# A Linformer attention and squared-ReLU network: attention visits spread over a batch's 56 steps, k and v projected a batch ahead, inverse rows in four buffers

## The chip, the cores and the metric

The kernel runs on one core of a Trainium2 chip. The metric is the device time of one execution in microseconds (us). Three runs of the kernel before gave 481.41, 481.42 and 482.23 us, a median of 481.42 us. One further execution was profiled; all lines of the profile are of that one. The engines are TensorE (PE, with its weight loads shown as PEld), VectorE (DVE), ScalarE (ACT), GpSimd (POOL) and SyncE (SP). The last two do little here but issue transfers; a "q" behind an engine's name marks its queue.

## What is computed

```python
batch, n_heads, seq, head_dim = (8, 8, 1024, 64)
k_proj = 64
...
k_proj = np.einsum('ks,bhsd->bhkd', E, k)
v_proj = np.einsum('ks,bhsd->bhkd', F, v)
scale = 1.0 / np.sqrt(q.shape[-1])
scores = scale * np.matmul(q, k_proj.transpose(0, 1, 3, 2))
scores = scores - np.max(scores, axis=-1, keepdims=True)
attn = np.exp(scores)
attn = attn / (np.sum(attn, axis=-1, keepdims=True) + 1e-09)
return np.matmul(attn, v_proj).astype(np.float32)
...
x = np.ascontiguousarray(attn_out.transpose(0, 2, 1, 3)).reshape(B * S, H * D)
...
h = np.maximum(x @ w_in, 0.0)
return (h * h @ w_out).astype(np.float32)
```

An attention over 64 projected keys for each of 8 batches and 8 heads gives an x of 8192 rows by 512. Two products follow, to 2048 columns with a squared ReLU and back to 512. Matmuls run in bf16.

## The kernel before

**Tiles.** A batch has 1024 rows of x, kept transposed as `xT`, and is worked off in two chunks of 512. The first product makes `h` from `xT` and `w_in`, the second makes the output from `h` and `w_out`. For batch 0 and the first product of chunk (1, 0) these are plain sums over four or sixteen blocks (`first_plain`, `second_cold`). All later ones are done in Strassen's way: seven products of half-size blocks instead of eight, with sums of blocks (`x_sum`, `s`, `w_in_sum`, `w_out_sum`) made on VectorE.

**A first product.** `Group` has one method for each of the seven products, p1 to p7. Each writes 4 matmuls of 128x256 into a PSUM bank. p1's result is copied by ACT (L677) to a second bank, `chain`, into which p6, p7 and p4 add. p5's and p6's results are copied to SBUF by ACT as tiles `u` (`keep`, L544), and p3 and p7 finish with a VectorE instruction, `relu_sum` (L666), that adds such a `u` to a bank. p2 and p4 finish with a ReLU on ACT (L662). In every second group VectorE also squares `h` and makes the sums `s`, all recorded through one helper line, L150. A group is seven steps. p4 of a group comes as the third step of the next one, so it stands three steps behind its own p7, whose `relu_sum` reads the bank that p4 adds into.

**A second product.** `second_spread` cuts the seven products into quanta of 4 matmuls (L572), one or two to a step, in banks `ps_second`. `put` takes a finished quarter to a tile `o_sb` (ACT's copy L562, or VectorE's addition in L150) and stores it from SyncE's queue (L566). Within 28 steps, puts stand at about 8 and 28 on ACT and 20 and 24 on VectorE. The last chunk runs `second_seven`; its last put is made in two halves, one by ACT (L562) and one by VectorE (L560).

**Steps.** From the second chunk of batch 1 on, `both` issues at each step one quantum of a first and one of a second product. A batch is 56 steps, and step t+1 of the loop over b begins at t = 56(b-1). What else TensorE does is put at a step with `at` or `on`, and is issued after that step's matmuls. TensorE's order is thus written out by hand (`tc.manual_schedule`). The other engines' orders are made by the framework's scheduler, and on each engine instructions run in that order.

**Attention, as visits.** `project` (L258, L259) multiplies k and v by E and F; VectorE and ACT copy the result to `kp` and `vp` (L246, L247, L251, L252). `transpose_k_dma` (L295) and `transpose_q_dma` (L321) are transposing DMAs from SyncE's queue. `scores` (L329) is followed by ACT's exponential (L343). `sums` (L363) adds up the exponentials of two pairs of heads, and ACT makes the inverse rows twice (L367 to L369); VectorE fills in the missing rows by copies (L373). `sums_spread` (L382) makes them once (L386, L387) into a tile `inv`, and eight DMAs (L393) from SyncE's queue copy them to two tiles `rs`. `values` (L405) is followed by two VectorE multiplications with `rs` into `xT` (L409). `sum_x` makes four x_sums. In the stage of 56-step batches all visits share one pair of PSUM banks, `ps_att`, so each waits for the one before to be read.

**Buffers.** `part` holds the tiles `u` in five buffers, `outp` the tiles `o_sb` in three, tag `rs` of `soft` has three. There is one buffer each for the loaded K, V and Q of a batch and for `qT`, and two for `kp`, `kT`, `vp` and `xT`. K, V and Q are loaded from GpSimd's queue (L89).

**Order of visits before, for the loop's b.** Scores 3 of batch b+1 at t+1, q transpose of b+2 at t+2, sums_spread 2 at t+3, values 0 to 3 at t+7, 10, 20 and 23, both sum_x at t+24; then for batch b+2: project at t+30, k transpose at t+32, scores 0 to 2 at t+44, 47 and 53, sums_spread 0 at t+50. K and V of b+3 are loaded from t+34.

Of the kernel before, what the change touches and what calls it, by code (L numbers as in the profile page):

```python
# [9 lines left out]
P = 128  # L10
# [9 lines left out]
def kernel(  # L20
# [19 lines left out]
    NI = 8  # L40
# [23 lines left out]
    part_pool = ctx.enter_context(tc.tile_pool(name="part", bufs=5))  # L64
    out_pool = ctx.enter_context(tc.tile_pool(name="outp", bufs=3))
# [31 lines left out]
    e_f32 = soft_pool.tile([KP, S], F32, tag="rs", name="e_f32")  # L97
    nc.sync.dma_start(e_f32[:], E[:])

    k_f32 = soft_pool.tile([P, 2, NI, D], F32, tag="rs", name="k_f32")  # L100
# [121 lines left out]
    class Attention:  # L222
# [123 lines left out]
        def inverse(self, ps):  # L346
            rs = soft_pool.tile([P, 2, TCH], F32, tag="rs", name="rs")
            nc.scalar.activation(rs[:], ps[:], AF.Ln)
            nc.scalar.activation(rs[:], rs[:], AF.Exp, scale=-1.0)
            return rs  # L350
# [6 lines left out]
        def sums(self, pr):  # L357
# [8 lines left out]
            rs = [soft_pool.tile([P, 2, TCH], F32, tag="rs", name="rs") for _ in range(2)]  # L366
# [9 lines left out]
        def sums_spread(self, pr):  # L376
# [8 lines left out]
            inv = soft_pool.tile([P, 2, TCH], F32, tag="rs", name="inv")  # L385
            nc.scalar.activation(inv[:], ps[:], AF.Ln)  # L386
            nc.scalar.activation(inv[:], inv[:], AF.Exp, scale=-1.0)  # L387
            for j in range(2):
                rs = soft_pool.tile([P, 2, TCH], F32, tag="rs", name="rs")
                for a in range(2):  # L390
                    have = 32 * (2 * a + j)
                    for to in (64 * a, 64 * a + 32):
                        nc.sync.dma_start(rs[to:to + 32], inv[have:have + 32])  # L393
# [44 lines left out]
    class Chunk:  # L438
# [103 lines left out]
        def keep(self, ps):  # L542
            u = part_pool.tile([P, DM], F32, name="u")
# [99 lines left out]
    class Group:  # L643
# [35 lines left out]
        def p5(self):  # L679
            self.other = bank(n=turn["bank"] + 2)  # L680
            self.product(5, self.other, True)
            self.kept5 = self.chunk.keep(self.other[:])

        def p6(self):
            self.product(6, self.chain)
            self.u2 = self.chunk.keep(self.chain[:])
# [21 lines left out]
    with tc.manual_schedule(engines={PE}):  # L708
# [81 lines left out]
        at(45, nxt.sums, 0)  # L790
        at(47, nxt.scores, 2)
        at(49, nxt.scores, 3)
        at(50, nxt.values, 0)
        at(52, nxt.values, 1)
        at(53, nxt.sums, 2)
# [11 lines left out]
        at(1, nxt.transpose_k)  # L807
        at(3, nxt.scores, 0)
        at(5, nxt.scores, 1)
        at(7, nxt.sums_spread, 0)  # L810
        at(9, nxt.scores, 2)
        at(11, nxt.scores, 3)
        turn["pairs"] = 1
        run_all(chunk[1, 0].first_plain())
# [45 lines left out]
        def on(step, b, name, *args):  # L860
            at(step, lambda: getattr(atts[b], name)(*args))

        for b in range(1, B - 1):
            t = 56 * (b - 1)
            if b > 1:
                on(t + 1, b + 1, "scores", 3)
            on(t + 3, b + 1, "sums_spread", 2)
            on(t + 7, b + 1, "values", 0)
# [52 lines left out]
```

## Time and profile before

| | |
|---|---|
| median of three runs | 481.42 us |
| the profiled execution | 482.35 us |
| its span, first to last instruction | 480.5 us |
| one batch of 56 steps (186.64 to 242.50 us) | 55.86 us |
| in it busy: PE, PEld, DVE, ACT | 55.57, 44.80, 43.43, 35.78 us |
| granted TensorE clock | 1.00 throughout |
| DMA, mean over the span | 139 GB/s |

The page lists for each engine its busy time, share of the span and instructions. Groups of instructions stand by source line, with the tile written, an arrow, and the tiles read; behind the bar come busy time, the mean of one in ns and the idle time before them with what ended it. The timeline has start, length, engine, line and tiles, and in brackets the idle time before the instruction and who ended it; matmuls that follow one another are merged ("x4"). The chain of waits goes back from the end, at each step to what released the work, and is shown in order of time. Matmul ends are modelled, so that distances between starts say more than idle times. All VectorE sums and squares carry the line L150 of their helper and are told apart by their tiles.

### The profile page before, as it was taken

Reading aid. Unit: us, or ns where it says so; the run is one execution under the profiler, and the core shown is the slowest. Engines: PE = TensorE matmul, PEld = TensorE weight load, DVE = VectorE, ACT = ScalarE, POOL = GpSimd, SP = SyncE. Lnnn points to the kernel's source line nnn. Section 1 sums busy time; section 2 is a strip of 40 time slices with the busy share of each in tenths; the row PEclk is TensorE's granted clock in tenths of the full one; section 3 lists DMA queues with packets and bytes.
Section 4 is the critical chain, followed back from the end, with each engine's and each line's share of the span. In section 5 each row is a group of like instructions: output and inputs, shape, how many; then the busy total and the mean of one; then the engine's idle time right before and its main releaser. Section 6 shows DMA issues by size and latency. Waiting matters only on the chain.

```text
span 480.5 us, 10027 instructions
## 1 busy us (share of the span) xinstructions
PE 470.4 (98%) x4106; PEld 351.5 (73%) x4106; DVE 350.7 (73%) x613; ACT 287.2 (60%) x466; POOL 32.4 (7%) x45
## 2 busy tenths in 40 slices
PE   8999999999999999999999999999999999999996
PEld 3444445537878788787878778887887778888885
DVE  2456897956996679767897579966797678967671
ACT  2464467397547774678546785477745775565641
POOL 7310010200010000100010000100000000000000
PEclk9999999999999999999999999999999999999999
DMA  9999998999949496767939499495811054101012
GB/s 184 204 205 206 221 164 150 168 230 189 197 86 168 122 201 163 119 134 186 196 103 182 93 220 175 96 160 139 203 56 55 23 132 111 67 23 67 24 65 89
DMA packets 80046, 66.98 MB, mean 139 GB/s; under 512 B 30720, under 2 KB 76032, under 8 KB 80000
## 3 DMA queue, kind: packets, MB, share of 16 engines
q0 software_dynamic: 30640, 29.23, 39.4%
q1 hardware_dynamic: 49216, 36.97, 29.2%
q8 instruction: 32, 0.52, 0.4%
q10 hardware_dynamic: 144, 0.13, 0.1%
q14 instruction: 14, 0.11, 0.1%
HBM read 59.24 MB, written 16.78 MB: 158 GB/s over the span
## 4 chain that ended last, share of the span: by engine, by line
PE 71%; DVE 22%; ACT 3%; issue 2%; DMA 1%; DVEq 0%; ACTq 0%
PE ps_bank L652 28%; PE ps_second L572 27%; PE ps_bank L489 6%; DVE h L150 3%; DVE x_sum L150 3%; DVE h L666 3%; DVE s L150 2%; PE ps_att L329 2%; DVE xT L409 2%; PE ps_second L549 2%; PE ps_att L405 2%; DVE kp L246 1%; DVE rs L373 1%; DVE kp L247 1%; DVE w_in_sum L150 1%
## 5 line engine op out<-in xcount | busy, mean ns | idle before, releaser
L150 DVE TENSOR_TENSOR h<-h 128x1024 bf16<-128x1024 bf16 (+1 forms) x182 | 108.0, 616 | 39.1 <-ACT h L662 25.4
L652 PE MATMUL ps_bank<-x_sum,w_in_sum 128*128 128x256 bf16 x624 | 93.9, 273 | 0.0
L652 PEld LDWEIGHTS <-w_in_sum 128*128 128x128 bf16 x832 | 78.7, 98 | 16.2 <-issue 7.5
L572 PEld LDWEIGHTS <-h 128*128 128x128 bf16 x832 | 80.8, 98 | 10.6 <-DVE h L150 0.2
L662 ACT ACTIVATE h<-ps_bank 128x512 bf16<-128x512 f32 x104 | 62.9, 605 | 28.5 <-PE ps_bank L652 28.3
L544 ACT COPY u<-ps_bank 128x512 f32<-128x512 f32 x107 | 63.2, 591 | 26.6 <-PE ps_bank L652 23.6
L666 DVE CUSTOM_DVE_ANT_0 h<-ps_bank,u 128x512 bf16<-128x512 f32 x104 | 68.9, 685 | 13.0 <-PE ps_bank L652 12.5
L652 PEld LDWEIGHTS <-w_in 128*128 128x128 bf16 x624 | 58.8, 98 | 16.2 <-issue 9.5
L677 ACT COPY ps_bank<-ps_bank 128x512 f32<-128x512 f32 x52 | 29.7, 570 | 66.1 <-PE ps_bank L652 66.1
L572 PEld LDWEIGHTS <-s 128*128 128x128 bf16 x624 | 61.0, 98 | 7.1
L652 PE MATMUL ps_bank<-xT,w_in 128*128 128x256 bf16 x416 | 62.5, 273 | 0.0
L572 PE MATMUL ps_second<-w_out_sum,s 128*128 128x256 bf16 x416 | 62.4, 273 | 0.0
L572 PE MATMUL ps_second<-w_out_sum,h 128*128 128x256 bf16 x416 | 62.2, 273 | 0.0
L572 PE MATMUL ps_second<-w_out,h 128*128 128x256 bf16 x416 | 60.3, 273 | 0.0
L409 DVE TENSOR_TENSOR xT<-ps_att,rs 128x512 bf16<-128x512 f32 x56 | 36.0, 684 | 15.9 <-PE ps_att L405 15.9
L489 PE MATMUL ps_bank<-xT,w_in 128*128 128x512 bf16 x192 | 45.3, 379 | 1.8 <-DVE xT L434 1.0
L485 ACT ACTIVATE h<-ps_bank 128x512 bf16<-128x512 f32 x48 | 28.1, 606 | 16.1 <-PE ps_bank L489 15.9
L150 DVE TENSOR_TENSOR o_sb<-ps_second,u 128x512 f32<-128x512 f32 x27 | 18.5, 684 | 25.9 <-PE ps_second L572 20.7
L489 PEld LDWEIGHTS <-w_in 128*128 128x128 bf16 x192 | 17.7, 98 | 24.6 <-issue 6.2
L343 ACT ACTIVATE expT<-ps_att 128x1024 bf16<-128x1024 f32 x32 | 32.9, 1036 | 2.9 <-PE ps_att L329 2.5
L652 PE MATMUL ps_bank<-x_sum,w_in 128*128 128x256 bf16 x208 | 31.4, 273 | 1.4 <-DVE h L666 1.4
L652 PE MATMUL ps_bank<-xT,w_in_sum 128*128 128x256 bf16 x208 | 31.3, 273 | 0.0
(104 smaller groups left out, 477.2 us busy)
## 6 DMA issues: line engine op xcount, KB each, us to landing
out_dram<-o_sb SPq DMA_DIRECT2D x63, 256.0 KB, 2.4
rs<-inv SPq DMA_DIRECT2D x96, 128.0 KB, 2.8
K_sb<-in_k_dram POOLq DMA_DIRECT2D x7, 1024.0 KB, 9.5
V_sb<-in_v_dram POOLq DMA_DIRECT2D x7, 1024.0 KB, 15.8
Q_sb<-in_q_dram POOLq DMA_DIRECT2D x7, 1024.0 KB, 12.6
w_out<-in_moe_w_out_dram POOLq DMA_DIRECT2D x4, 512.0 KB, 17.9
w_in<-in_moe_w_in_dram POOLq DMA_DIRECT2D x3, 512.0 KB, 15.0
k_f<-in_k_dram SPq DMA_DIRECT2D x1, 512.0 KB, 4.9
```

Source lines behind the costliest of these rows:

```text
L150: return nc.vector.tensor_tensor(out=o, in0=x, in1=y, op=op)
L329: nc.tensor.matmul(ps[o, par], lhsT=self.kT[r, h % 4, h // 4, :], rhs=self.qT[r, h, n, :], start=True, stop=True)
L343: nc.scalar.activation(e[:], ps[:], AF.Exp, scale=SCALE)
L409: nc.vector.tensor_tensor(out=self.xT[:, pr, :, par], in0=ps_x[par].rearrange("p (c t) -> p c t", c=2), in1=rs[:, par].rearrange("p (c t) ...
L485: nc.scalar.activation(h, ps.rearrange("p (a t) -> p a t", a=2), AF.Relu)
L489: nc.tensor.matmul(ps[:], lhsT=w_in_blk(cb, fb), rhs=self.xT[:, cb, self.c].rearrange("p a t -> p (a t)"), start=(cb == 0), stop=(cb == NC ...
L544: nc.scalar.copy(u[:], ps)
L572: nc.tensor.matmul(ps[:, i * HM:(i + 1) * HM], lhsT=self.h_form(n, fb)[:, i * P:(i + 1) * P], rhs=w_out_form(n, fb), start=fresh and i == ...
L652: nc.tensor.matmul(ps[:, j * HC:(j + 1) * HC], lhsT=w_in_form(n, cb, 2 * self.g + j), rhs=self.chunk.x_form(n, cb), start=fresh and j == 0 ...
L662: nc.scalar.activation(self.out(kh, a), ps[:], AF.Relu)
L666: nc.vector._custom_dve(TENSOR_ADD_SAT, out=self.out(kh, a), in0=ps[:], in1=more[:], s0=3.0e38, s1=0.0)
L677: nc.scalar.copy(self.chain[:], self.first[:])
```

## The change

The attention visits of a batch move to other steps, with a short sequence of their own for batch 1. `project` of batch b+3 (instead of b+2) now comes in the pass of b, at t+37, with its k transpose and the load of the next K and V at t+38. Scores 0 and 1 of b+2 go to t+22 and t+25, sums_spread 0 to t+28, scores 2 and 3 to t+34 and t+42, values 0 and 1 to t+47 and t+50, sums_spread 2 to t+54, all in the pass before the one in which they stood or earlier in it. Values 2 and 3 go to t+8 and t+19. The two sum_x stand at t+23 and t+33. The q transpose goes from t+2 to t+43. In the stage before the loop, sums 0 of batch 1 becomes a `sums_spread` whose copies go half to SyncE's and half to GpSimd's queue, and the visits of batch 2 move by one to two steps. Tag `rs` gets four buffers, `outp` two, and `part` two for each of two tags: "first" for the u of first products, "second" for those of second ones.

```diff
--- before.py
+++ after.py
@@ -61,8 +61,8 @@
     soft_pool = ctx.enter_context(tc.tile_pool(name="soft", bufs=3))
     x_pool = ctx.enter_context(tc.tile_pool(name="x", bufs=2))
     form_pool = ctx.enter_context(tc.tile_pool(name="form", bufs=1))
-    part_pool = ctx.enter_context(tc.tile_pool(name="part", bufs=5))
-    out_pool = ctx.enter_context(tc.tile_pool(name="outp", bufs=3))
+    part_pool = ctx.enter_context(tc.tile_pool(name="part", bufs=2))
+    out_pool = ctx.enter_context(tc.tile_pool(name="outp", bufs=2))
     psum = ctx.enter_context(tc.tile_pool(name="ps", bufs=1, space=bass.MemoryType.PSUM))
     turn = {"att": 0, "bank": 0, "pairs": 2}
 
@@ -94,10 +94,10 @@
         return t
 
 
-    e_f32 = soft_pool.tile([KP, S], F32, tag="rs", name="e_f32")
+    e_f32 = soft_pool.tile([KP, S], F32, tag="rs", name="e_f32", bufs=4)
     nc.sync.dma_start(e_f32[:], E[:])
 
-    k_f32 = soft_pool.tile([P, 2, NI, D], F32, tag="rs", name="k_f32")
+    k_f32 = soft_pool.tile([P, 2, NI, D], F32, tag="rs", name="k_f32", bufs=4)
     nc.sync.dma_start(k_f32[:], tokens(k, 0, h=slice(0, 2)))
 
     K0, Q0, V0 = (qkv_pool.tile([P, H, NI, D], BF16, name=n) for n in ("K_sb", "Q_sb", "V_sb"))
@@ -344,7 +344,7 @@
             return e
 
         def inverse(self, ps):
-            rs = soft_pool.tile([P, 2, TCH], F32, tag="rs", name="rs")
+            rs = soft_pool.tile([P, 2, TCH], F32, tag="rs", name="rs", bufs=4)
             nc.scalar.activation(rs[:], ps[:], AF.Ln)
             nc.scalar.activation(rs[:], rs[:], AF.Exp, scale=-1.0)
             return rs
@@ -363,7 +363,7 @@
                     nc.tensor.matmul(
                         ps[c:c + 32, par], lhsT=ones[r, 0:32], rhs=self.e[pr + j][r, par], start=True, stop=True
                     )
-            rs = [soft_pool.tile([P, 2, TCH], F32, tag="rs", name="rs") for _ in range(2)]
+            rs = [soft_pool.tile([P, 2, TCH], F32, tag="rs", name="rs", bufs=4) for _ in range(2)]
             nc.scalar.activation(rs[1][:], ps[:], AF.Ln)
             nc.scalar.activation(rs[0][:], rs[1][:], AF.Exp, scale=-1.0)
             nc.scalar.activation(rs[1][:], rs[1][:], AF.Exp, scale=-1.0)
@@ -373,7 +373,7 @@
                     nc.vector.tensor_copy(rs[j][lack:lack + 32], rs[j][have:have + 32])
                 self.rs[pr + j] = rs[j]
 
-        def sums_spread(self, pr):
+        def sums_spread(self, pr, queues=(nc.sync, nc.sync)):
 
             ps = att_psum()
             for j in range(2):
@@ -382,15 +382,15 @@
                     nc.tensor.matmul(
                         ps[c:c + 32, par], lhsT=ones[r, 0:32], rhs=self.e[pr + j][r, par], start=True, stop=True
                     )
-            inv = soft_pool.tile([P, 2, TCH], F32, tag="rs", name="inv")
+            inv = soft_pool.tile([P, 2, TCH], F32, tag="rs", name="inv", bufs=4)
             nc.scalar.activation(inv[:], ps[:], AF.Ln)
             nc.scalar.activation(inv[:], inv[:], AF.Exp, scale=-1.0)
             for j in range(2):
-                rs = soft_pool.tile([P, 2, TCH], F32, tag="rs", name="rs")
+                rs = soft_pool.tile([P, 2, TCH], F32, tag="rs", name="rs", bufs=4)
                 for a in range(2):
                     have = 32 * (2 * a + j)
                     for to in (64 * a, 64 * a + 32):
-                        nc.sync.dma_start(rs[to:to + 32], inv[have:have + 32])
+                        queues[j].dma_start(rs[to:to + 32], inv[have:have + 32])
                 self.rs[pr + j] = rs
 
         def values(self, pr, spare=False):
@@ -539,8 +539,8 @@
                         yield
 
 
-        def keep(self, ps):
-            u = part_pool.tile([P, DM], F32, name="u")
+        def keep(self, ps, tag="second"):
+            u = part_pool.tile([P, DM], F32, name="u", tag=tag)
             nc.scalar.copy(u[:], ps)
             return u
 
@@ -679,11 +679,11 @@
         def p5(self):
             self.other = bank(n=turn["bank"] + 2)
             self.product(5, self.other, True)
-            self.kept5 = self.chunk.keep(self.other[:])
+            self.kept5 = self.chunk.keep(self.other[:], "first")
 
         def p6(self):
             self.product(6, self.chain)
-            self.u2 = self.chunk.keep(self.chain[:])
+            self.u2 = self.chunk.keep(self.chain[:], "first")
 
         def p2(self):
             self.product(2, self.first)
@@ -787,12 +787,12 @@
         at(44, nxt.transpose_q, 2)
         at(44, nxt.transpose_q, 3)
         at(44, lambda: atts[2].load_q())
-        at(45, nxt.sums, 0)
-        at(47, nxt.scores, 2)
-        at(49, nxt.scores, 3)
-        at(50, nxt.values, 0)
-        at(52, nxt.values, 1)
-        at(53, nxt.sums, 2)
+        at(45, nxt.sums_spread, 0, (nc.sync, nc.gpsimd))
+        at(48, nxt.scores, 2)
+        at(50, nxt.scores, 3)
+        at(51, nxt.values, 0)
+        at(53, nxt.values, 1)
+        at(54, nxt.sums, 2)
         at(59, nxt.values, 2)
         at(60, nxt.values, 3)
         at(60, chunk[1, 1].sum_x)
@@ -804,13 +804,16 @@
         run_all(chunk[0, 0].first_cold(), chunk[0, 0].second_cold(), chunk[0, 1].first_plain(), chunk[0, 1].second_seven(*(bank()[:] for _ in range(3))))
 
         nxt = atts[2]
-        at(1, nxt.transpose_k)
-        at(3, nxt.scores, 0)
-        at(5, nxt.scores, 1)
-        at(7, nxt.sums_spread, 0)
-        at(9, nxt.scores, 2)
-        at(11, nxt.scores, 3)
+        at(2, nxt.transpose_k)
+        at(4, nxt.scores, 0)
+        at(6, nxt.scores, 1)
+        at(10, nxt.scores, 2)
+        at(13, nxt.scores, 3)
         turn["pairs"] = 1
+        def on(step, b, name, *args):
+            at(step, lambda: getattr(atts[b], name)(*args))
+
+        on(8, 2, "sums_spread", 0)
         run_all(chunk[1, 0].first_plain())
         lent.close()
         second_pool = ctx.enter_context(tc.tile_pool(name="ps_second", bufs=1, space=bass.MemoryType.PSUM))
@@ -857,33 +860,39 @@
                 next(s, None)
                 yield
 
-        def on(step, b, name, *args):
-            at(step, lambda: getattr(atts[b], name)(*args))
-
+        def project(step, b):
+            on(step, b, "project")
+            on(step + 1, b, "transpose_k_dma")
+            if b + 1 < B:
+                at(step + 1, begin, b + 1)
+                on(step + 1, b + 1, "load_kv")
+
+        on(6, 2, "sums_spread", 2)
+        on(10, 2, "values", 0)
+        on(12, 2, "values", 1)
+        project(15, 3)
         for b in range(1, B - 1):
             t = 56 * (b - 1)
-            if b > 1:
-                on(t + 1, b + 1, "scores", 3)
-            on(t + 3, b + 1, "sums_spread", 2)
-            on(t + 7, b + 1, "values", 0)
-            on(t + 10, b + 1, "values", 1)
-            on(t + 20, b + 1, "values", 2)
-            on(t + 23, b + 1, "values", 3)
+            on(t + (20 if b == 1 else 8), b + 1, "values", 2)
+            on(t + (23 if b == 1 else 19), b + 1, "values", 3)
             for c in range(2):
-                at(t + 24, lambda b=b, c=c: chunk[b + 1, c].sum_x())
+                at(t + 23 + 10 * c, lambda b=b, c=c: chunk[b + 1, c].sum_x())
             if b + 2 < B:
-                on(t + 2, b + 2, "transpose_q_dma")
+                if b == 1:
+                    on(t + 12, b + 2, "transpose_q_dma")
+                on(t + (25 if b == 1 else 22), b + 2, "scores", 0)
+                on(t + (27 if b == 1 else 25), b + 2, "scores", 1)
+                on(t + (30 if b == 1 else 28), b + 2, "sums_spread", 0)
+                on(t + 34, b + 2, "scores", 2)
                 if b + 3 < B:
-                    at(t + 2, begin, b + 3)
-                    on(t + 3, b + 3, "load_q")
-                on(t + 30, b + 2, "project")
-                on(t + 32, b + 2, "transpose_k_dma")
+                    on(t + 20, b + 3, "load_q")
+                    project(t + 37, b + 3)
+                on(t + 42, b + 2, "scores", 3)
                 if b + 3 < B:
-                    on(t + 34, b + 3, "load_kv")
-                on(t + 44, b + 2, "scores", 0)
-                on(t + 47, b + 2, "scores", 1)
-                on(t + 50, b + 2, "sums_spread", 0)
-                on(t + 53, b + 2, "scores", 2)
+                    on(t + 43, b + 3, "transpose_q_dma")
+                on(t + 47, b + 2, "values", 0)
+                on(t + 50, b + 2, "values", 1)
+                on(t + 54, b + 2, "sums_spread", 2)
         steps = both()
         run(steps)
         assert not plan, plan
```

## The prediction

> **What bounds the kernel now.** I read the page's busy shares first, then the waits of TensorE, then the chain of waits and the timeline where those waits stand, then the queues of SyncE and GpSimd.
>
> ```profile
> PE 470.4 (98%) x4106; PEld 351.5 (73%) x4106; DVE 350.7 (73%) x613; ACT 287.2 (60%) x466; POOL 32.4 (7%) x45
> PE ps_bank L652 <- DVE h L666: 1.4, 5, 0.3
> 200.47 0.70 DVE h L666
> 201.18 0.04 issue
> 201.22 0.60 PE ps_bank L652 x4
> ...
> 255.75 0.60 PE L652 MATMUL ps_bank<-x_sum,w_in_sum 128*128 128x256 bf16 x4
> 256.19 0.60 PE L572 MATMUL ps_second<-w_out,h 128*128 128x256 bf16 x4
> 257.07 0.60 PE L652 MATMUL ps_bank<-x_sum,w_in 128*128 128x256 bf16 x4 [0.28 <-DVE h L666]
> ```
>
> TensorE is the bound: from 109 us on its groups of four matmuls start 0.44 us apart, and only the idle between them can be won. In each batch one distance is 0.88 instead (256.19 to 257.07), so 0.44 us is lost, more than the 0.28 shown as idle, because matmul ends are modelled. It occurs at 145, 201, 257, 313 and 368 us: five times, 2.2 us. The chain says why: from the values at 186.6 to 201.2 it runs on VectorE without a break (values, both x_sums, o_sb, the k casts), so the `relu_sum` of p7 ends late and p4, which adds into the bank that it reads, waits.
>
> ```profile
> 75.72 1.38 DVE L373 COPY rs<-rs 32x1024 f32<-32x1024 f32 x2
> 75.75 0.28 PE L549 MATMUL ps_bank<-w_out,h 128*128 128x256 bf16 x1 [0.47 <-DVE h L150]
> 81.34 0.41 PE L363 MATMUL ps_att<-expT,ones 64*32 64x512 bf16 x8 [0.20 <-DVE xT L409]
> 93.64 0.40 PE L288 MATMUL ps_bank<-ident,kp 128*128 128x128 bf16 x4 [0.21 <-DVE kp L247]
> 70.27 0.87 POOL L89 DMA_DIRECT2D Q_sb<-in_q_dram  x1 [8.76 <-PE ps_bank L314]
> ```
>
> Between 75 and 105 us the same engine holds TensorE up in smaller pieces. From distances of starts: 0.64 at 75.7 (seven matmuls from 74.35 reach 75.11), 0.30 at 78 (a product of 16 takes 2.21, its neighbours 1.91), 0.27 at 81.3, 0.35 at 93.6, 0.15 at 104: 1.7 us. The L373 copies and the third ACT pass (L369) are in the middle of it.
>
> ```profile
> out_dram<-o_sb SPq DMA_DIRECT2D x63, 256.0 KB, 2.4
> rs<-inv SPq DMA_DIRECT2D x96, 128.0 KB, 2.8
> 223.91 4.61 SPq L321 DMA_TRANSPOSE qT<-Q_sb  x1
> 216.52 6.12 SPq L393 DMA_DIRECT2D rs<-inv  x8
> 475.06 0.69 DVE L150 TENSOR_TENSOR o_sb<-ps_bank,u 128x512 f32<-128x512 f32 x1 [1.00 <-PE ps_bank L549]
> 476.85 0.37 ACT L562 COPY o_sb<-ps_second 128x256 f32<-128x256 f32 x1 [4.70 <-PE ps_second L549]
> 477.26 0.42 DVE L560 COPY o_sb<-ps_second 128x256 f32<-128x256 f32 x1 [1.50 <-ACT o_sb L562]
> ```
>
> These are the queues and the tail that the change touches: a q transpose holds SyncE for 4.6 us, eight copies of inverse rows for 6.1 us, and after the last matmul there is only ACT's, then VectorE's copy and their stores.
>
> **What the Trainium skill says.** "Perfetto Trace Analysis", section Identifying the Most-Contended Engine, calls matmul busy time no measure of headroom; here the 98% hides the 0.44 us distances, so it agrees. The same page, section Per-engine timelines, has ACT and VectorE strictly in order: an instruction that waits holds all behind it; the unbroken VectorE chain fits. "DMA: Bandwidth & Descriptors", section Queues, rings and completion order, says that each DMA engine takes turns between queues, packet by packet, and consumes one queue in order. The trace agrees: with the k transpose running beside the k and v loads, 258 to 262 us, 130 to 170 packets per us pass in either queue, against 1130 of a q transpose alone (227 to 229 us) and 190 to 200 of the loads alone.
>
> **Part 1, spreading the visits (batches 2 to 5).** No matmul is added or removed. Before, VectorE got between steps 20 and 31 of a batch the values 2 and 3 (four L409 at 0.65), two x_sums (8 at 0.42), two o_sb (0.68), the project casts (4 at 0.38 and 0.69) and the odd group's burst: 2.6+3.3+1.4+2.2 = 9.5 us on top of a Strassen load of 7.7 us per 14 steps. After, values 2 stand at 8, values 3 at 19, one x_sum at 23, the other at 33, project at 37, values 0 and 1 at 47 and 50. I walked VectorE's order with these durations against steps of 0.875 us plus 0.45 for an attention visit and 1.96 for project. From 19 to 28 it has 1.3+1.4+1.4+1.7+0.6+1.3+0.7 = 8.4 us of work in 8.8 us. The p7 result of step 28 is read 1.3 us after that step, p4 starts 2.2 us after: 0.9 us to spare. Groups ending at 14, 21, 35, 42, 49 come out with 1 us or more. All four waits go: 4 x 0.44 = -1.8 us. Project casts end 2.4 us after project, scores 3 follow 4.4 us after.
>
> **Part 2, batch 1.** Here project stands at 15 and values 2 and 3 at 20 and 23, and VectorE's order puts both L409 of values 2 ahead of the p7 `relu_sum` of step 21. The walk ends that at 24.5 us after step 0 against a p4 start at 24.3, and values 3 at 26.5 against scores 0 at 26.1: some 0.45 us lost, what batch 1 loses now. Bounds -0.45 to +0.6; I take 0.
>
> **Part 3, sums to sums_spread at step 45.** It removes four L373 (2.75 us of VectorE) and one L369 (1.06 of ACT) and adds four 128 KB copies on SyncE and four on GpSimd. So the 1.7 us go if the copies land in time. inv stands at 73.8 us; SyncE's four are issued by 76.2 and land by about 79 (2.8 each), near values 0. GpSimd's four stand in their queue behind the Q load issued at 70.27, whose packets end at 79 now and about 80 with SyncE's copies in between; 0.5 MB at 200 KB per us puts them at 82, and values 1 (matmul at about 79.5) waits on VectorE till then. Behind it wait the L373 copies of sums 2 (83.7 to 86.5), then o_sb, for which product 4 waits about 0.45 us. -1.7+0.45 = -1.25. No run shows that queue: landing at 81 gives -1.7, each us after 82 costs one, 84.5 gives +1.2.
>
> **Part 4, two output buffers.** In the loop an o_sb waits for the store of two puts earlier, 7 us before at the closest. At the end the very last copy (L560, 477.26) takes the buffer of the o_sb of 475.06, whose store the trace has issued at 475.78 and landed at 477.88. So L560 goes from 477.26 to 477.95: +0.7 on the last store. Bounds 0.5 to 1.2.
>
> **Part 5, edits at nothing.** Two buffers for each tag of u: p5's copy waits for the p7 `relu_sum` of the group before, which in the walk ends 0.2 to 1.2 us sooner in batches 2 to 5; without that cover ACT waits, but p3 reads the bank four steps later. Four rs buffers: inv and its copies find old values consumed. load_kv at 38 is needed 55 steps on. Both cover the same thing if late: TensorE.
>
> Sum: -1.8+0-1.25+0.7 = -2.35. The profiled execution took 482.35 us (span 480.5, 1.85 around it), 0.9 over the median of 481.42. It would become 480.0, the median 479.1.
>
> **Rivals.**
> *The waits move.* VectorE's load of 43.4 us in 55.8 is the same, and where its order puts an L409 ahead of a `relu_sum`, as in batch 1, 0.45 us comes back each time. With it in all batches and the tail: 481.42-1.25+0.7 = 480.9. Against it: 0.9 us to spare in the walk.
> *GpSimd's copies are late* (84.5): -1.8+1.2+0.7 = +0.1, 481.5.
> *The q transpose holds SyncE* (slower). Step 43 puts it among the K and V loads, for batches 1 to 3; before, at step 2, it ran alone in 4.6 us. At 150 packets per us each, the loads' 2048 packets end 15 us after project, and by then only some 700 of the transpose's 4096 have passed; it ends at 18.5, and SyncE is held till about 17. Behind it stand two stores and the copies of sums_spread 2 (inv at 19 to 20.5). The o_sb of step 57 needs the first store, which then lands at 20; ACT reaches that copy at 19.4 to 20.4. First inverse rows land at 25.6, values 2 at 25.4. So it fits, with some 2.4 us before p3 and the p4 square are late. If the transpose takes 4 us longer than this, each of three batches loses about 1.6 us: 479.1+4.8 = 483.9. From 2.4 us of lateness it decides.
>
> **How the numbers follow.** As planned 0.62 (477.9 to 480.3, from the bounds of parts 2 to 4), waits move 0.13, GpSimd late 0.07, SyncE held 0.18. The predicted time is the first, 479.1. Leaving out the outer half of the last and the best tenth of the first, the range is 477.7 to 482.8. 0.2% of 481.4 is 0.96, about what can be told from no change: faster below 480.46: 0.63; within: 0.18; slower above 482.38: 0.19.
>
> **What would show it.** Right: no 0.88 distance from 165 us on, p4 never waiting for L666; no idle at 75 and 81 us; L560 waiting for a store at the end. Wrong: a qT transpose of over 12 us on SyncE with ACT waiting at o_sb; values 1 at 80 us waiting for a DMA beyond 84; L652 waits for L666 in later batches.

## The result: 3.0% slower, and where it went in the profile

The changed kernel takes 496.35 us (median) against 481.83 for the kernel before, measured beside it: 1.0302 times as long, 95% interval 1.0269 to 1.0335. The forecast was 479.1. The profiled execution took 495.74 us, its span 494.0, against 480.5 before.

The page first, its line of busy shares and its row of the granted TensorE clock (40 slices of 12.35 us, a 9 is 90% or more):

```profile
PE 471.8 (96%) x4106; PEld 352.8 (71%) x4106; DVE 346.2 (70%) x609; ACT 286.5 (58%) x465; POOL 34.6 (7%) x49
PEclk9999998899999999999999999999999999999999
```

The number of matmuls is the same and TensorE is busy 1.4 us longer, but the span grew by 13.4: TensorE stands idle. VectorE and ScalarE even have less to do. And the clock row has two slices below 9, from 74 to 99 us.

To find the places I took the start of the same matmul in both traces at the borders of the stages, and the growth of the difference from one border to the next. The first 20 us are the same program in all kernels here; what they add (-1.4 to +2.8) is scatter between executions.

| stage (times of before) | after - before, us |
|---|---|
| to the first first-layer matmul, 20 us | -0.67 |
| to 82.5 us (the sums of batch 1 in between) | -1.64 |
| ahead of the sums of pairs 2 and 3, 82.5 | +5.26 |
| second product of batch 0 from there, to 92.3 | +2.32 |
| first chunk of batch 1, to 109.2 | +2.32 |
| batch 1 | +5.02 |
| batches 2, 3, 4 | +1.53, +0.86, +1.78 |
| batches 5 and 6 | -4.34 |
| behind the last matmul | +1.00 |
| sum | +13.4 |

Two of these numbers hold moved work, which is neither gain nor loss. The sums of pairs 2 and 3 stand one step later than before and so fall behind the border at 82.5: 0.44 of the -1.64 and 0.44 of the +5.26 are this visit's own time, so that the small waits gained 1.2 and the stop lost 4.8. And of batch 1's 5.02, 3.8 are work that was moved there (a project and four visits, 1.96 + 4 x 0.45 by the forecast's own prices) and that comes back as most of the -4.34 of batches 5 and 6. What is left are four losses: ahead of and behind 82.5 us, in batch 1's chunks, in batches 2 to 4 and at the end. TensorE's waits (total, times, longest, in us) name the first three:

```profile
PE ps_att L363 <- DVE xT L409: 4.5, 1, 4.5
PE ps_bank L652 <- ACT u L544: 3.0, 5, 1.0
PE ps_bank L288 <- DVE kp L247: 1.4, 1, 1.4
...
PE ps_second L572 <- ACT ps_second L588: 1.2, 3, 0.4
PE ps_att L329 <- DMA kT<-kp: 1.2, 1, 1.2
...
PE ps_bank L652 <- DVE h L666: 0.2, 1, 0.2
```

The last line is the wait that the change was to remove: five times 0.3 before, once 0.2 now. That worked. The lines above it are new, but for the one of L288, which was 0.2 before.

**The front.** The timeline around 73 to 85 us (start, duration, engine, line; in brackets the idle time ahead and what ended it):

```profile
73.17 2.91 SPq L393 DMA_DIRECT2D rs<-inv  x4
73.43 2.00 POOL L393 DMA_DIRECT2D rs<-inv  x4 [2.96 <-ACT inv L387]
...
83.61 2.48 DVE L409 TENSOR_TENSOR xT<-ps_att,rs 128x512 bf16<-128x512 f32 x4 [6.38 <-DMA rs<-inv]
84.96 0.63 PE L363 MATMUL ps_att<-expT,ones 64*32 64x512 bf16 x8 [4.53 <-DVE xT L409]
```

SyncE has issued its four copies of inverse rows by 76.1 us, but they land only at 80.2 to 83.4, and VectorE's first multiply, which needs these four, starts at 83.6. It frees the PSUM pair for which the next sums wait, so TensorE stands still for 4.5 us. The clock then falls, as the busy time by stretches shows (the last three columns are the granted clock, the DMA share and GB/s):

```profile
core 0: us, PE busy (x) PEld busy (x) DVE busy (x) ACT busy (x) POOL busy (x), PEclk, DMA share, GB/s
80.00:84.90 4.90, 0.42 (x4) 0.13 (x2) 1.28 (x3) 0.59 (x1) 0.00 (x0) 0.85 0.87 215
84.90:90.30 5.40, 5.34 (x31) 3.53 (x32) 2.99 (x6) 3.23 (x4) 0.93 (x1) 0.50 0.65 145
90.30:97.00 6.70, 6.70 (x61) 4.25 (x60) 3.28 (x5) 0.39 (x1) 0.00 (x0) 1.00 1.00 165
```

Between 84.9 and 90.3 us the clock is 0.50 and only 31 matmuls run. The busy time of 5.34 hides it: a matmul at half clock is simply busy for longer. The Trainium skill, "TensorE: Matmul & The Clock Gate", section Part 1: The HAM clock gate, has the clock at half after about 3.4 us of idle and back after about as much work; this trace agrees in kind, with 4.5 us of idle and, by the clock record, 6.8 us at half, the start of it within the idle. Three later runs fell to half sooner than the page's figure, after 2.3 to 2.6 us of idle (e3, e1 and e8); there the measurement decides.

**The loop.** Around 160 to 182 us (batch 2; batch 4 looks the same):

```profile
159.64 1.87 SPq L295 DMA_TRANSPOSE kT<-kp  x1
162.90 14.81 SPq L321 DMA_TRANSPOSE qT<-Q_sb  x1
177.83 1.01 SPq L566 DMA_DIRECT2D out_dram<-o_sb  x2
...
180.56 0.59 ACT L562 COPY o_sb<-ps_second 128x512 f32<-128x512 f32 x1 [2.99 <-PE ps_bank L652]
181.68 0.60 PE L652 MATMUL ps_bank<-xT,w_in_sum 128*128 128x256 bf16 x4 [0.79 <-ACT u L544]
```

The q transpose holds SyncE for 14.8 us where it took 4.6 before. Two stores wait behind it until 177.8, ScalarE's copy into o_sb waits for a store to give a buffer back, and ScalarE works in order, so the copies of u that TensorE needs are late. The bracket of the copy names TensorE, which had long been done; the first of the two stores landed at 180.4, just ahead of the copy. In batch 4 the bracket of the same copy names the store:

```profile
294.89 0.59 ACT L562 COPY o_sb<-ps_second 128x512 f32<-128x512 f32 x1 [3.24 <-DMA out_dram<-o_sb]
```

**The first chunk of batch 1.** Here too an output copy waits for a store, but no store is held up in SyncE's queue:

```profile
88.97 0.93 POOL L89 DMA_DIRECT2D Q_sb<-in_q_dram  x1 [13.54 <-DMA qT<-Q_sb]
97.54 0.69 DVE L150 TENSOR_TENSOR o_sb<-ps_bank,u 128x512 f32<-128x512 f32 x1 [3.48 <-DMA out_dram<-o_sb]
99.80 0.59 ACT L562 COPY o_sb<-ps_bank 128x512 f32<-128x512 f32 x1 [9.11 <-DMA out_dram<-o_sb]
```

The first store of this stage is issued at 89.76, as soon as its tile is written, and lands at 97.35, 7.6 us later, beside the load of Q that GpSimd issued at 88.97. Only then can VectorE's o_sb of 97.54 start, and the kp for which L288 waits is made behind it.

**The end.** VectorE's last copy waits for the store of the buffer two puts back, as forecast:

```profile
490.47 0.42 DVE L560 COPY o_sb<-ps_second 128x256 f32<-128x256 f32 x1 [2.23 <-DMA out_dram<-o_sb]
```

### The profile page after: what moved, and what is told of

It reads as the page before. It is cut to its first block, busy times and chain, and to the rows that moved or that the text cites. A ratio compares the mean times of both kernels' runs of the same rounds, so it can differ in the third digit from the quotient of the medians.

```text
span 494.0 us, 10110 instructions
## 1 busy us (share of the span) xinstructions
PE 471.8 (96%) x4106; PEld 352.8 (71%) x4106; DVE 346.2 (70%) x609; ACT 286.5 (58%) x465; POOL 34.6 (7%) x49
## 4 chain that ended last, share of the span: by engine, by line
PE 75%; DMA 14%; DVE 6%; ACT 3%; issue 1%; SPq 0%; DVEq 0%; ACTq 0%; POOLq 0%
PE ps_bank L652 31%; PE ps_second L572 30%; DMA Q_sb<-in_q_dram 4%; PE ps_bank L489 3%; DMA out_dram<-o_sb 3%; DMA w_in<-in_moe_w_in_dram 3%; PE ps_att L329 2%; PE ps_att L258 2%; DMA kT<-kp 2%; DMA rs<-inv 2%; PE ps_att L405 2%; PE ps_bank L549 1%; PE ps_second L549 1%; DMA K_sb<-in_k_dram 1%; DVE w_out_sum L150 1%
## 5 line engine op out<-in xcount | busy, mean ns | idle before, releaser
L652 PEld LDWEIGHTS <-w_in_sum 128*128 128x128 bf16 x832 | 78.1, 98 | 21.9 <-issue 13.4
L572 PEld LDWEIGHTS <-h 128*128 128x128 bf16 x832 | 81.4, 98 | 11.4 <-issue 1.9
L572 PEld LDWEIGHTS <-s 128*128 128x128 bf16 x624 | 61.1, 98 | 7.0
L572 PE MATMUL ps_second<-w_out_sum,s 128*128 128x256 bf16 x416 | 62.4, 273 | 0.0
L572 PE MATMUL ps_second<-w_out_sum,h 128*128 128x256 bf16 x416 | 62.2, 273 | 0.0
L572 PE MATMUL ps_second<-w_out,h 128*128 128x256 bf16 x416 | 60.1, 272 | 1.2 <-ACT ps_second L588 1.2
```

The costliest lines, as they stand in the source:

```text
L572: nc.tensor.matmul(ps[:, i * HM:(i + 1) * HM], lhsT=self.h_form(n, fb)[:, i * P:(i + 1) * P], rhs=w_out_form(n, fb), start=fresh and i == ...
L652: nc.tensor.matmul(ps[:, j * HC:(j + 1) * HC], lhsT=w_in_form(n, cb, 2 * self.g + j), rhs=self.chunk.x_form(n, cb), start=fresh and j == 0 ...
```

## The experiments

Three theories came out of this, for three parts of the change that the forecast had priced apart: (1) the inverse-row copies land late beside a load in flight, TensorE idles and loses its clock; (2) the q transpose among the K and V loads holds SyncE; (3) two output buffers turn a late store into a stall. In the column "gap" of the next table, 0.44 is the visit that stands a step later, in every kernel with the new steps 48 to 54. The kernels' growth against before by stage, in us; the last column is the median of the runs, with 481.8 to 482.4 for before beside them:

| kernel | to 82.5 | gap | to 92.3 | first chunk | batch 1 | 2, 3, 4 | 5 and 6 | end | median |
|---|---|---|---|---|---|---|---|---|---|
| after | -1.64 | +5.26 | +2.32 | +2.32 | +5.02 | +1.53 +0.86 +1.78 | -4.34 | +1.00 | 496.35 |
| e1 sums back | -0.28 | +0.44 | +0.59 | +3.69 | +4.49 | +1.29 +1.16 +1.60 | -4.34 | +0.76 | 491.95 |
| e2 q behind | -1.66 | +5.46 | +2.28 | +3.12 | +5.71 | -0.50 -0.50 -0.50 | -4.34 | +0.99 | 491.09 |
| e3 three outputs | -1.65 | +6.52 | +1.88 | +0.15 | +5.77 | +3.61 -0.33 -0.50 | -4.34 | +0.24 | 490.09 |
| e4 SyncE only | -1.65 | +3.69 | +3.11 | +2.15 | +5.30 | +3.28 +0.94 +3.40 | -4.34 | +0.75 | 496.86 |
| e5 Q load behind | -1.25 | +1.88 | +0.01 | +3.14 | +5.25 | +1.71 +0.89 +1.70 | -4.34 | +0.99 | 491.45 |
| e6 three together | -0.28 | +0.44 | +0.41 | -0.44 | +5.72 | -0.50 -0.50 -0.50 | -4.34 | 0 | 482.23 |
| e8 two of them | -0.23 | +0.44 | +0.41 | +3.82 | +4.62 | -0.50 -0.50 -0.50 | -4.34 | +0.76 | 486.14 |
| c3 | 0 | 0 | 0 | -0.44 | +8.09 | -0.50 -0.50 -0.50 | -4.34 | 0 | 485.51 |
| c2 | 0 | 0 | 0 | -0.43 | +5.40 | -0.50 -0.50 -0.50 | -4.34 | 0 | 481.53 |
| c4 | 0 | 0 | 0 | -0.44 | +5.28 | -0.50 -0.50 -0.50 | -4.34 | 0 | 481.14 |
| e7 before, two outputs | +0.37 | 0 | 0 | +1.54 | 0 | 0 0 0 | 0 | +0.78 | 485.89 |

**e1: the old form of the sums at step 45.**

```diff
-        at(45, nxt.sums_spread, 0, (nc.sync, nc.gpsimd))
+        at(45, nxt.sums, 0)
```

> The kernel after, with the inverse rows of pairs 0 and 1 of batch 1 copied within VectorE at step 45 again, as before the change, instead of by eight DMAs. Theory 1 (the eight copies land late beside the Q load of batch 2; VectorE's multiply waits, TensorE idles 4.5 us and its clock falls): the TensorE idle of 4.5 us ahead of the sums of pairs 2 and 3 and the stretch at half clock both go (5.3 + 2.3 us of the ledger), the small waits of the old form come back (1.6 us): 490.4 us, and as low as 488 if the late stores at the start of the next chunk go too. Rival (the visits put one step later at 48 to 54 make the gap): the gap stays and the time is above 494.

491.95 us, 1.0205 times before (1.0187 to 1.0224). The gap and the slow clock behind it are gone, as theory 1 has it: of 7.58 us there remain 1.03, of which 0.44 is the moved visit. The rival falls, since the later visits are all still there. It is 1.5 us above what I expected, because the first chunk of batch 1 now loses 3.7 us where it lost 2.3. The copy that TensorE waits for there, and its waits, from the timeline and the list of waits of e1:

```profile
86.40 0.87 POOL L89 DMA_DIRECT2D Q_sb<-in_q_dram  x1 [15.24 <-DMA qT<-Q_sb]
97.12 0.58 ACT L562 COPY o_sb<-ps_bank 128x512 f32<-128x512 f32 x1 [10.52 <-DMA out_dram<-o_sb]
PE ps_bank L489 <- ACT o_sb L562: 2.5, 1, 2.5
```

ScalarE waits 10.5 us for a store before it can fill an output buffer. That store was issued at 89.2, at once when its tile was ready, and landed at 97.0, beside the load of Q. TensorE's 2.5 us of idle are followed by 3.4 us at half clock (98.1 to 101.5). So with the gap ahead of it gone, late stores cost more here; that one stall had covered part of the other fits this, but no run separates the two.

**e2: the q transposes of batches 4 to 7 behind the inverse-row copies.**

```diff
-                        queues[j].dma_start(rs[to:to + 32], inv[have:have + 32])
+                        self.copied = queues[j].dma_start(rs[to:to + 32], inv[have:have + 32])
...
+        def q_behind(b):
+            with tc.issue_after(atts[b + 2].copied.ins):
+                atts[b + 3].transpose_q_dma()
...
-                if b + 3 < B:
-                    on(t + 43, b + 3, "transpose_q_dma")
...
                 on(t + 54, b + 2, "sums_spread", 2)
+                if b + 3 < B:
+                    at(t + 54, lambda b=b: q_behind(b))
```

> The kernel after, with the q transposes of batches 4 to 7 queued on SyncE behind the inverse-row copies of step 54, when the K and V loads of the next batch have landed, instead of right behind the kT transpose at step 43. Theory 2 (the transpose beside the K and V loads holds SyncE for some 15 us, so stores are issued late and ScalarE's and VectorE's output copies wait for a buffer): the transposes take under 7 us on SyncE, the stalls of 2.1, 1.4 and 2.3 us in batches 2 to 4 go, 490.6 us (490 to 492.5). Rival (two output buffers alone make the stalls): stalls stay, 494.5 to 497.

491.09 us, 1.0183 times before (1.0157 to 1.0208). SyncE's queue in the same stretch of e2:

```profile
161.38 1.85 SPq L295 DMA_TRANSPOSE kT<-kp  x1
172.85 3.47 SPq L566 DMA_DIRECT2D out_dram<-o_sb  x2
178.62 5.29 SPq L393 DMA_DIRECT2D rs<-inv  x8
184.02 4.18 SPq L321 DMA_TRANSPOSE qT<-Q_sb  x1
```

The transpose takes 4.2 us instead of 14.8, and all three batches are now 0.50 us faster than before, with two output buffers and two for u still in place. So moving the transpose is enough to end the stalls of the loop, and what the change was meant to win there, 0.50 per batch, appears. The move does two things at once, it takes the transpose out from among the loads and puts it behind the copies; which of them counts isn't separated.

**e3: three output buffers, three for inverse rows.**

```diff
-    out_pool = ctx.enter_context(tc.tile_pool(name="outp", bufs=2))
+    out_pool = ctx.enter_context(tc.tile_pool(name="outp", bufs=3))
...
-                rs = soft_pool.tile([P, 2, TCH], F32, tag="rs", name="rs", bufs=4)
+                rs = soft_pool.tile([P, 2, TCH], F32, tag="rs", name="rs")
```

> The kernel after with three output buffers instead of two; to make room, three buffers instead of four for the inverse rows. Theory 3 (two output buffers are what turns a late store into a stall, at the start of batch 1's first chunk, in batches 2 to 4 and at the end): all waits of output copies for a store under 1 us, 496.4 - 2.3 (start of that chunk) - 4 to 5 (batches) - 1 (end) = 488 to 490. If SyncE's hold is longer than the third buffer covers: 492 to 494. If the fourth inverse-row buffer matters, a new wait of ScalarE's inverse for a values product appears and some of this is lost.

490.09 us, 1.0167 times before (1.012 to 1.0215). The first chunk loses 0.15 instead of 2.32 and the end 0.24 instead of 1.00, which is theory 3. ScalarE still waits 7.7 us for a store in the first chunk, more than the 1 us forecast, but TensorE no longer waits for it. In batches 3 and 4 the third buffer covers SyncE's hold. In batch 2 it doesn't, at least in the profiled execution, which was the slowest of the four (493.66; the others took 487.73 to 490.13). Its timeline shows a second customer of that queue:

```profile
162.97 14.53 SPq L321 DMA_TRANSPOSE qT<-Q_sb  x1
...
179.10 5.70 SPq L393 DMA_DIRECT2D rs<-inv  x8
...
189.90 1.29 DVE L409 TENSOR_TENSOR xT<-ps_att,rs 128x512 bf16<-128x512 f32 x2 [7.05 <-DMA rs<-inv]
```

The inverse-row copies stand behind the transpose too; with the stores no longer the first to be late, VectorE's multiply waits 7 us for them and TensorE 2.3 us for VectorE, with 3.4 us at half clock behind it. Here a third output buffer hides a blocked queue for the stores alone.

**e4: all eight copies on SyncE.**

```diff
-        at(45, nxt.sums_spread, 0, (nc.sync, nc.gpsimd))
+        at(45, nxt.sums_spread, 0, (nc.sync, nc.sync))
```

> The kernel after with all eight copies of the inverse rows of step 45 on SyncE's queue, none on GpSimd's. Theory 1 (the copies share the DMA engines with the Q load already in flight, whichever queue they are on): SyncE issues eight at about 0.73 us each from 73.2 to 79 us, the last lands at 84 to 86 us; 496 to 498 us. Rival (only GpSimd's queue is late, because its copies stand behind the Q load there): SyncE's land by 81 us, the gap and the slow clock go, about 489 us.

496.86 us, 1.0288 times before (1.0252 to 1.0324): no difference from after that these runs can tell (494.92 to 499.24 against 495.74 to 497.88). SyncE's copies and TensorE's wait in e4:

```profile
74.15 5.17 SPq L393 DMA_DIRECT2D rs<-inv  x8
PE ps_att L363 <- DVE xT L409: 3.2, 1, 3.2
```

They land 6.8 to 7.4 us after issue, on a queue that has nothing else in it. The forecast had thought GpSimd's queue the cause; it isn't. Whichever queue the copies take, they are late while the Q load runs.

**e5: the Q load of batch 2 behind GpSimd's copies.**

```diff
-        at(44, lambda: atts[2].load_q())
...
+        def q_load_behind():
+            with tc.issue_after(atts[1].copied.ins):
+                atts[2].load_q()
+
         at(45, nxt.sums_spread, 0, (nc.sync, nc.gpsimd))
+        at(45, q_load_behind)
```

> The kernel after with one thing moved: the Q load of batch 2 is queued on GpSimd behind its four inverse-row copies of step 45 instead of ahead of them, so that no load is in flight when the copies are issued. Theory 1 (the load in flight is what makes the copies land late): they land by about 77 us, the 4.5 us idle and the half clock go; the load then runs from about 75 to 89 us instead of 70 to 84, so the q transpose of batch 2 and the stores behind it on SyncE come some 5 us later and part of the gain is lost again at the start of batch 1's first chunk: 489 to 492 us. Rival (copies by DMA are slow here whatever else moves): the copies still land after 82 us and the gap stays, 495 to 498.

491.45 us, 1.0202 times before (1.0177 to 1.0227). The gap shrinks from 5.26 to 1.88, 1.44 without the moved visit, and the clock stays up, as the same stretch of e5 shows:

```profile
84.90:90.30 5.40, 5.40 (x52) 3.44 (x52) 4.47 (x7) 0.64 (x1) 0.00 (x0) 1.00 0.68 152
```

52 matmuls at clock 1.00 instead of 31 at 0.50. The copies land 2.4 to 5.2 us after issue (7.0 to 9.8 in after). So the load in flight is the cause, as theory 1 has it. And the price comes out where it was expected: the later Q load delays the q transpose, which here does hold up a store: its tile was ready at 84.6, it is issued at 90.5. The first chunk loses 3.14:

```profile
86.31 4.09 SPq L321 DMA_TRANSPOSE qT<-Q_sb  x1
90.51 4.12 SPq L566 DMA_DIRECT2D out_dram<-o_sb  x4
```

**e7: the kernel before with two output buffers.**

```diff
-    out_pool = ctx.enter_context(tc.tile_pool(name="outp", bufs=3))
+    out_pool = ctx.enter_context(tc.tile_pool(name="outp", bufs=2))
```

> The kernel before with two output buffers instead of three, nothing else. Theory 3 (two buffers cost where stores are late; before, stores are late only at the end and perhaps at the start of batch 1's first chunk): +0.8 to +1.2 at the end, 0 in batches 2 to 6, 0 to 2.5 at the start of that chunk: 482.5 to 485.5 us. Rival (two buffers make the stalls of batches 2 to 4 whatever the transposes do): 486 or more.

485.89 us, 1.0085 times before (1.0069 to 1.0102). Nothing in batches 1 to 6, 0.78 at the end, and 1.54 in the first chunk, where e7's timeline has the wait of e1 again:

```profile
94.61 0.59 ACT L562 COPY o_sb<-ps_bank 128x512 f32<-128x512 f32 x1 [9.72 <-DMA out_dram<-o_sb]
95.25 1.02 PE L489 MATMUL ps_bank<-xT,w_in 128*128 128x512 bf16 x4 [1.39 <-ACT o_sb L562]
```

The profiled execution (483.58) is the quickest of its runs. The others have a mean clock of 0.994 to 0.999 instead of 1.000. A longer wait here, with half clock behind it, would fit the four with 0.994 to 0.996: e1 and e8 show 3.4 us of half clock after waits of 2.5 and 2.6 us at this place. It doesn't fit the two with 0.998 and 0.999, which are as slow (485.73 and 486.81), so why these runs are slower than the profiled one stays open.

**e6 and e8: the corrections together.** e6 is e1, e2 and e3 in one kernel, e8 e1 and e2 alone.

> The kernel after with the three corrections together: inverse rows of pairs 0 and 1 of batch 1 copied on VectorE again, q transposes behind the inverse-row copies of step 54, three output buffers (and three for inverse rows). If the three theories are right and add up by place: front +0.8 against before, start of batch 1's first chunk +0.2, batch 1 +5.0 (3.7 of it work moved there), batches 2 to 4 -1.5, batches 5 and 6 -4.3, end 0: 0.2 above before, 481.5 to 482.5 us. If a cause is missing, 484 or more.

> The kernel after with two corrections, inverse rows of pairs 0 and 1 of batch 1 copied on VectorE and q transposes behind the copies of step 54, but still two output buffers and four for inverse rows. Theory 3: against the three corrections (482.2 us), +2.5 us at the start of batch 1's first chunk, +0.8 at the end, nothing in batches 2 to 6: 485 to 486 us. Rival (with the queues in order two buffers suffice): 482.2 to 483.

e6: 482.23 us, 0.9998 times before (0.9985 to 1.0011), the expected time: the three causes add up and none is missing at that size. e8: 486.14, 1.007 (1.0051 to 1.009), 3.9 us above e6, its trace has +3.82 in the first chunk, where e6 has -0.44, and 0.76 at the end. Two of its executions took 480.7 and the others 484.9 to 487.7, which would fit a close race for that store; no trace of one of the two shows it. With three buffers (e6) all twelve lie between 480.9 and 483.0.

**c3, c2, c4: what is left in batch 1.** e6 still loses 1.9 us there (5.72 less the 3.8 moved). Its waits have 1.0 us for the kT transpose and 0.8 for ScalarE's inverse. All three kernels are e6 with the front's visits back at their old steps 47 to 53, and in batch 1:

```diff
-                on(t + (25 if b == 1 else 22), b + 2, "scores", 0)
-                on(t + (27 if b == 1 else 25), b + 2, "scores", 1)
-                on(t + (30 if b == 1 else 28), b + 2, "sums_spread", 0)
+                on(t + (27 if b == 1 else 22), b + 2, "scores", 0)
+                on(t + (29 if b == 1 else 25), b + 2, "scores", 1)
+                on(t + (32 if b == 1 else 28), b + 2, "sums_spread", 0)
```

c3 also has `on(13, 2, "sums_spread", 2)` instead of step 6; c4 instead has values 0 and 1 at 11 and 13.

> The same three corrections and two more: the front's visits at their old steps 47 to 53, and in batch 1 the scores of pairs 0 and 1 of batch 3 and their sums two steps later (27, 29, 32), so that they do not wait for the kT transpose, with the sums of pairs 2 and 3 of batch 2 at step 13, behind the values that free their buffers. Front 0, start of the chunk +0.2, batch 1 +3.7 (moved work alone), batches 2 to 4 -1.5, batches 5 and 6 -4.3: 1.9 below before, 480 us. If the kT wait is not what batch 1 lost, 481.5 or more.

c3 took 485.51 us, 1.007 (1.0049 to 1.0091): a miss. From its queue and its waits:

```profile
123.79 5.50 SPq L393 DMA_DIRECT2D rs<-inv  x8
129.39 1.57 SPq L295 DMA_TRANSPOSE kT<-kp  x1
PE ps_att L329 <- DMA kT<-kp: 2.2, 1, 2.2
```

By moving the sums I had put their eight copies straight ahead of the kT transpose in SyncE's queue. It landed 10.3 us after issue (8.6 in e6), and the scores that I had moved by two steps waited longer than before.

> The kernel of the three corrections (482.2 us), with the front's visits at their old steps 47 to 53 and, in batch 1, scores of pairs 0 and 1 of batch 3 and their sums two steps later (27, 29, 32); the sums of pairs 2 and 3 of batch 2 stay at step 6. Theory 4 (in batch 1 the scores come too early for the kT transpose, whose packets queue behind copies and stores): its wait of 1.0 us and the 1.2 us excess ahead of these scores go, and the front's 0.6 us: 480.4 us. Rival (kT lands later again, as it did behind the eight copies of step 13): 482 us or more.

> As the one before, and in batch 1 the values of pairs 0 and 1 of batch 2 one step later (11 and 13 instead of 10 and 12). The wait of 0.8 us of the values product for ScalarE's inverse, which stands behind an output copy, goes: 0.9 us less, 479.5 us, below the kernel before by 2.5 us or more. Rival (VectorE's multiplies now crowd the casts of project at step 15): as the one before or slower, 480.4 to 482.

c2: 481.53 us, 0.9983 (0.9971 to 0.9995). The kT wait is gone, but batch 1 falls by 0.3 us only, not by 1.2; in its place comes `PE ps_second L572 <- ACT ps_second L588`, of 0.8 (after had such waits too). c4: 481.14 us, 0.9984 (0.997 to 0.9997). The wait for the inverse goes and the expected rival takes most of it, project's matmul behind VectorE's multiply. c4's waits of TensorE show both:

```profile
PE ps_second L572 <- ACT ps_second L588: 0.8, 1, 0.8
PE ps_att L258 <- DVE xT L409: 0.7, 1, 0.7
```

c2 and c4 can't be told from each other. Both are faster than before by about 0.2%, 0.8 and 1.2 us by the medians where 1.9 and 2.8 were expected; the rest of what batch 1 loses found a new place to wait each time.

## Why the prediction was wrong, step by step

The forecast summed to -2.35, the profile has +13.4. Of the difference, parts 3 and 4 with what they set off make up most: +5.9 up to 92.3 us where -1.25 stood, and +3.3 in the first chunk and at the end where +0.7 stood. Batches 1 to 6 come to +4.9 where -1.8 stood.

- **Part 1, the spreading (-1.8).** Right, and a little more: 0.50 per batch in batches 2 to 4 (e2, e6, c2, c4), where 0.44 was forecast, and about as much in batch 5 (2.43 less 1.96 for the project that it no longer has). In after itself the gain is there too and is covered by the stall of the rival below.
- **Part 2, batch 1 (0, at most +0.6).** Off: about 1.2 us are lost (5.02 less 3.8). The walk followed VectorE; what came last was the kT transpose, 1.2 us of waiting, since scores 0 stand ten steps behind project and the transpose lands 8.8 us after its issue when K and V loads start beside it. The step never asked when that DMA lands. It isn't the whole loss either: c2 took this wait away and won 0.3.
- **Part 3, sums_spread at step 45 (-1.25).** The step that failed first. That the small waits would go was right: 1.2 up to 82.5 us, as its own three terms up to there say (0.64, 0.30 and 0.27). The landing times were not: SyncE's copies were to land at 79 us, 2.8 us after issue, by the median of copies that run mostly without a load beside them. The last of them landed at 83.4, 8.1 us after its issue, GpSimd's at 83.1 to 84.6. The forecast named contention for GpSimd's queue only, and e4 shows that this queue isn't the point. Its price, one us for each us after 82, was too small by kind: the multiply holds the PSUM pair, TensorE stands still, and then runs at half clock, so 4.8 + 2.3 us for copies of SyncE that landed 4.4 us later than forecast. The rival "GpSimd's copies are late" had the place right, but not the copies: the multiply that TensorE waited for needs SyncE's. It gave this 1.2 us and a chance of 0.07.
- **Part 4, two output buffers (+0.7).** The end came out at 1.00 (0.78 in e7). The term left out is the start of batch 1's first chunk, 2.3 us in after, up to 3.8 when the gap ahead of it is gone. The step said "in the loop an o_sb waits for the store of two puts earlier, 7 us before at the closest"; it didn't look at the puts at the end of batch 0. Their stores run beside the loads of Q, K and V of batch 3: in before, three of the four already land 7.5 to 8.8 us after their issue, and a third buffer covers it. That the loads make these stores late is read from the traces; no run was made to test it. It fits e5, where the load of Q comes only at 92.5 us: the two stores ahead of it land 2.4 us after issue, the two behind it 8.2 and 9.8.
- **Part 5 (0).** No run shows a cost of the tags of u: e2 and e6 have them and lose nothing in the loop. The fourth inverse-row buffer wasn't tried alone.
- **The rival "the q transpose holds SyncE" (0.18).** This is what happened in the loop, with its mechanism as described. Its sign came true too, a transpose of over 12 us with ScalarE waiting at o_sb. It had SyncE free 17 us after project and 2.4 us to spare from there. The transposes end 19.7, 17.7 and 19.2 us after project's last matmul in batches 2, 3 and 4, and cost 2.0, 1.4 and 2.3 us (the growths plus the 0.50 won), where it priced 1.6 for 4 us of lateness. What failed is the spare time: in batch 3, with SyncE only 0.7 us later than estimated, ScalarE's copy already waits 2.3 us for its store. So the hold was estimated well, the spare time was not there, and the chance of 0.18 was too small.

The sum was made of parts that each looked at one engine or one queue. Most losses have in them the landing time of a small DMA beside a load, and the trace of before had such times. The copies of inverse rows that it issues from 103.1 us, beside a load of V, land 5.3 to 7.0 us after issue, and the later ones beside a load of Q (118.7 to 121.8) 7.1 to 7.7. The k transposes beside K and V loads take 8.5 to 9.0 us to land, the one without a load 2.3. The prediction looked at one of these, from 258 to 262 us, for its packets and not for its landing. The view of these copies in before gives the 2.8 with its spread (shortest, median, longest):

```profile
DMA to landing us min/median/max: 2.2/2.8/8.9
```

## What to carry to other kernels

Take the landing time of a DMA from rows in which the same other traffic runs, not from the median: 2.8 us were 7 to 10 beside a load, and the profile of before had rows of 5 to 8 to warn of it. When a large DMA moves, list what stands behind it in its queue (here stores and copies), and who waits for each; a buffer more hides only one of them. And a TensorE wait of more than about 2 us has to be priced with the clock behind it.

## What the runs showed of the hardware

- The clock: the granted clock was at half for 6.8 us around idles of 4.5 to 5.8 us (after, e2, e3) and for 3.4 us after idles of 2.3 to 3.2 us (e3, e1, e8, e4). It stayed at 1.00 after 2.2 us in c3 and 1.4 us in e5. The length of one idle doesn't settle it: in e4 it fell at 184.3 and 300.4 us with no single idle above 1.1 us there. In the records every stretch at half that ends before the kernel does is 3.41 us or twice that. Worked out from the traces: in the 3.4 us ahead of each fall behind 70 us, TensorE had been idle for 50 to 99% of the time, and no fall followed a slice that was idle for less. The border is rough, since matmul ends are modelled: one slice with 55% (e5, from 91.0 us) had no fall, one with 50% (e4, from 180.9 us) had one.
- A DMA transpose of 1 MB (qT) held SyncE 12.9 to 14.8 us among K and V loads (after) and 4.2 us without (e2), although the loads are on GpSimd's queue.
- Copies of 128 KB issued while a Q load of GpSimd ran landed 7.0 to 8.1 us after issue from SyncE's queue and 9.6 to 9.8 from GpSimd's (after), against 2.4 to 5.2 with the load moved behind them (e5). In after the first packets of the copies went out at 77.9 us, 4.7 us after the first issue. Where that time goes before the first packet is not settled by these runs.
